# Attention and gated feed-forward on one core: values products in three bursts a pair, output copies a unit later, small writes and one multiplication moved on GpSimd

## Chip, cores and metric

One Trainium2 chip, one core of it. The metric is device time of one execution in microseconds (us), as the median of several runs; lower is better. TensorE is PE in the profile, VectorE DVE, ScalarE ACT, GpSimd POOL, and SyncE, which issues the DMAs, SP.

## What is computed

The reference, cut to what matters (4 batches, 8 heads, 576 positions, head size 64, all float32):

```python
scores = scale * q @ k.T + bias            # bias from a small network on relative positions
attn   = exp(scores - max); attn /= sum
x      = attn @ v                           # heads side by side: (4, 576, 512)
h      = relu(x @ w_in)
conv   = sum_k conv_w[k] * h shifted by k   # three taps along the sequence
out    = (h * sigmoid(conv)) @ w_out
```

## The kernel before, in words

Three stages follow each other: the bias network (until about 65 us), attention (65 to 297 us), and the feed-forward part. Nothing reorders the work: each engine runs its instructions in the order in which the Python code issues them, and waits on semaphores where data or a buffer is not ready.

Attention works on **pairs** n = 0 to 15: two heads of one batch. A pair has five **units**, 0 to 4, one for each tile of queries (`t`, in the loop also `ui`); unit 0 holds the first 64 queries of both heads, units 1 to 4 hold 128 queries of each head. The main loop counts all units as `u`. In one turn of it, the steps belong to three different units, so that each engine has work ahead:

- PE multiplies the scores of unit u + 2, one head after the other (`scores`, L349), into two PSUM buffers that take turns (`psS`). DVE adds the bias, takes the row minimum of the negated sum and writes it to SBUF (`reduce`, L360, with a small read of the accumulator, `nm`). A score buffer is free again when its reduction is done, and the second head's also serves, in units 1 to 4, for a few transposes (`side_transposes`, L408; L412 turns the row sums) that DVE copies out.
- ACT exponentiates unit u + 1 (`expo`, L374). After that `turned_sp` (L328) writes two columns of the same SBUF buffer under its second name `sr`, so that the next tenant of the buffer, three units on, has something to wait for.
- PE transposes unit u (`transposes`, L420), the two row halves of the tile into two of three PSUM buffers (`psT`). ACT copies one out, DVE the other (lines L88 and L91): into `ptx` for units 0 to 2 (X, 320 columns), into `pty` for units 3 and 4 (Y, 256 columns).
- PE multiplies the transposed tile with the values (`pv_parts`, L457). X and Y of a pair are five parts each, of two matmuls each, in one PSUM buffer (`psO`); the trace has two records for each matmul. The queue `fill` holds the parts, and `pv_share` says how many parts unit 0, 1, 2, 3 and 4 run after their transposes. Y of a pair is ready after its unit 4, so it is worked off in units 0 to 2 of the next pair; X in units 3 and 4. The last part of X or Y copies the output from PSUM to the tile `x` (ACT, L88).

Beside this, weights for the second part are narrowed: a raw tile is loaded, in odd `u` DVE shifts one word right (L97) and ACT scales the other (L99), in even `u` DVE joins them (L103) and POOL splits the result in two (L131, L132). Once a pair POOL multiplies the output of the pair before last by the inverse sums (`apply_norm`, L497), which come back from memory as the tile `rb`.

The lines that say how the parts are shared and what the last part does:

```python
pv_share = (2, 2, 1, 3, 2)
...
parts = len(fill) if u < 5 else pv_share[ui]
while fill and parts > 0:
    fill.popleft()()
    parts -= 1
...
if ui == 2 and n > 1:
    apply_norm(n - 2)
```

Of the kernel before, what the change touches and what calls it, by code (L numbers as in the profile page):

```python
# [9 lines left out]
F32 = mybir.dt.float32  # L10
F32R = mybir.dt.float32r
I32 = mybir.dt.int32
AF = mybir.ActivationFunctionType
# [6 lines left out]
def attention_ffn_kernel(  # L20
# [11 lines left out]
    nc = tc.nc  # L32
    B, S, DM = out.shape
    NP = qk.shape[1]
# [4 lines left out]
    P = 128  # L39
# [30 lines left out]
    x_p = pool(ctx, "x", B)  # L70
# [16 lines left out]
    def act(o, i):  # L87
        nc.scalar.activation(o, i, AF.Copy)  # L88
# [45 lines left out]
    with tc.manual_schedule():  # L134
# [134 lines left out]
        def bias_out(blk):  # L269
            nf, nr = reach(blk)  # L270
            n = max(nf, nr + 1)
            ps = bias_ps.pop(blk)
            st = sts[blk // 2 % 5].rearrange("p (b n) -> p b n", b=2)
            if n > 512:
                o, i = st[:, blk % 2:blk % 2 + 1], ps.rearrange("p (b a) x -> p b (a x)", b=1)
            else:
                o, i = st, ps
            fwd = nf > nr


            if n > 512 or blk % 2:
                k = relu_from(blk) - 3
                for oo, ii in (
                    (slice(nr, nr + nf), slice(0, nf)) if fwd else (slice(0, nr + 1), slice(nr, None, -1)),
                    (slice(0, nr), slice(nr, 0, -1)) if fwd else (slice(nr + 1, nr + nf), slice(1, nf)),
                ):
                    nc.scalar.activation(o[:, :, oo], i[:, :, ii], AF.Identity, bias=kv[:, k:k + 1], scale=inv_scale)  # L287
            if blk % 2 == 0:
                return
            at = 64 + (blk - 1) * P * BW - nr  # L290
            dst = bias_d[at:at + 2 * P * BW].rearrange("(b p c) -> p b c", b=2, c=BW)
            nc.sync.dma_start(dst[:, :, 0:nr + nf], st[:, :, 0:nr + nf])
# [14 lines left out]
        xb = {0: x0}  # L307
# [17 lines left out]

        def turned_sp(n, t):
            tile = sp_p.tile([P, 2 * S + 2], F32R, name="sr", tag=spt[n, t][1])
            nc.scalar.activation(tile[:, 2 * S:], pars[:, 0:2], AF.Copy)  # L328
            spt[n, t] = (tile, None)


# [105 lines left out]

        ops_t = {}
        waiting = {}

        def pv_parts(n, g):
            p, b = seq[n]

            waiting[n] = waiting.get(n, 0) + 1
            x0, width = (XW, YW) if g else (0, XW)

            def part(c):
                pt, vt = ptt[n, g], vts[n]
                if c == 0:
                    ops_t[n, g] = psO.tile([P, 512], F32, name="o")  # L450
                po = ops_t[n, g]
                for h in range(2):
                    if c == 4:
                        slot, blk = (9 if h else 4), 4
                    else:
                        slot = blk = 5 + c if h else c
                    nc.tensor.matmul(  # L457
                        po[D * h:D * h + D, 0:width], vt[:, slot, :], pt[:, blk, :],
                        start=(c == 0), stop=(c == 4),
                    )  # L460
                if c == 4:
                    del ptt[n, g]
                    waiting[n] -= 1
                    if b not in xb:
                        xb[b] = x_p.tile([P, NP, S], F32, name=f"x{b}", tag="x")
                    act(xb[b][:, p, x0:x0 + width], po[:, 0:width])

            return [lambda c=c: part(c) for c in range(5)]

        def invert(n):  # L470
            sm, r = sms.pop(n), rr_t[n % 2][:, 0:9]
            nc.vector.tensor_scalar(r, sm, 1e-9, None, op0=ALU.add)
            nc.vector.reciprocal(r, r)
# [120 lines left out]
        for i in range(NBLK):  # L594
            nxt = bias_hidden(i + 1) if i + 1 < NBLK else None
            bias_mm(i, hidden)
            if last:
                bias_out(*last)
            last = (i,)
            hidden = nxt  # L600
            if i % 8 == 6 % 8 and i >= 6:
                load_bias(0, (i - 6) // 8)
            if i == 1:
                load_v(0)
            if i == 16:
                load(1)
            if i == 20:
                load_v(1)
            if i % 8 == 13 % 8 and i >= 13:
                unit = unit_steps(*first[(i - 13) // 8])  # L610
            if unit:
                next(unit, None)
            if fill:
                fill.popleft()()
        bias_out(*last)
        load_bias(0, 4)
        while fill:
            fill.popleft()()
        for _ in unit:
            pass  # L620
        for u in range(2):
            for h in heads(flat[u][1]):
                reduce(scores(*flat[u], h), *flat[u], h)
            if u == 0:
                for h in heads(flat[0][1]):
                    expo(*flat[0], h)
                turned_sp(*flat[0])
        pv_share = (2, 2, 1, 3, 2)
        hs_ff = {}
        raw_w = {}  # L630
        job_steps = iter(())
# [3 lines left out]
        for u, (n, t) in enumerate(flat):  # L635
            p, b = seq[n]
            ui = units.index(t)
            sums = n - 1 if ui == 2 and n else None
            side = None
            if u + 2 < NU:  # L640
                for h in heads(flat[u + 2][1]):
                    if side is not None:
                        reduce(side, *flat[u + 2], 0)
                    side = scores(*flat[u + 2], h)
            if t:
                if side is None:
                    side = psS.tile([P, 2, 512], F32, name="s")
                side_transposes(side, n, t, sums)
            if u + 2 < NU:
                reduce(side, *flat[u + 2], h)  # L650
            if u + 1 < NU:
                for h in heads(flat[u + 1][1]):
                    expo(*flat[u + 1], h)
                turned_sp(*flat[u + 1])
            transposes(n, t, side, sums)
            next(job_steps, None)

# [4 lines that stand above are left out]
            next(job_steps, None)  # L662
            del spt[n, t]
            if u + 2 >= NU:
                f = u + 2 - NU
                hs_ff[0, f] = ffn_in(0, f)
            if u == 1 or n and ui == 2 and n + 2 < NSEQ:
                load(2 if u == 1 else n + 2)
            if u in conv_weights:
                conv_weights[u]()  # L670

            for at, do in ((u - 7, "load"), (u - 11, "split")):
                job = at // 2
                if at % 2 == 0 or not 0 <= job < 4 * KC + 2 * FE:
                    continue
                if job < 4 * KC:
                    src, dst = w_in[job // 4 * P:job // 4 * P + P], wi[job // 4]
                else:
                    src, dst = w_out[(job - 4 * KC) // 2 * P:(job - 4 * KC) // 2 * P + P], wo[(job - 4 * KC) // 2]
                cs = slice(job % 4 * 256, job % 4 * 256 + 256) if job < 4 * KC else slice(job % 2 * 256, job % 2 * 256 + 256)  # L680
                if do == "load":
                    raw_w[job] = (e_p if job % 3 else woe_p).tile([P, 256, 2], I32, name="raw_w", tag="h")
                    load_w(raw_w[job], src[:, cs])
                else:
                    job_steps = split_w_steps(e_p, dst[:, :, cs], raw_w.pop(job), ("cv", "cv"))
            if u + 2 < NU:
                n2, t2 = flat[u + 2]
                p2, b2 = seq[n2]
                if b2 == B - 1 and p2 + 1 < NP:
                    load_bias(p2 + 1, t2)  # L690
            if ui == (0 if n > 1 else 1) and n > 0:
                invert(n - 1)
            if ui == (2 if n > 1 else 3) and 1 <= n and n + 1 < NSEQ:
                load_v(n + 1)
            if ui == 3 and n > 0:
                store_sums(n - 1)
            if ui == 4 and n > 0:
                spread_sums(n - 1)
            if ends_group(n, t):
                fill.extend(pv_parts(n, t > 2))  # L700

            if ui == 2 and n > 1:
                apply_norm(n - 2)
            if n == NSEQ - 2 and ui > 1:
                x_parts(0, ui - 2)
            if n == NSEQ - 1 and ui == 0:
                x_parts(0, 3)
            if n == NSEQ - 1 and ui in (1, 2):
                load_wo(FE - 1 + ui)
        while fill:  # L710
            fill.popleft()()
        invert(NSEQ - 1)
        turn_sums(NSEQ - 1)
        apply_norm(NSEQ - 2)
# [200 lines left out]
```

## Time and profile before

| | |
|---|---|
| three runs | 502.59 us median, 502.55 to 504.32 |
| profiled execution, its own time | 501.91 us |
| its span, first to last instruction | 500.1 us |
| mean granted TensorE clock | 0.998 of full speed |
| PE, weight loads, DVE, ACT, POOL busy | 96%, 70%, 77%, 62%, 21% of the span |
| attention, 150 to 200 us: PE, DVE, ACT, POOL busy in 50 us | 49.57, 44.97, 42.44, 15.10 us |
| DMA engines' mean share in that stretch | 0.80 |
| chain that ended last | PE 87%, DVE 5%, ACT 5% |

The busy share of PE is no measure of how much of PE is used, since matmuls are pipelined and their ends are modelled. What can be read well is the start of each group: the time from one start to the next is what a group costs where PE doesn't wait. The sum of the profiled execution is made against its own 501.91 us, which lies 0.68 us under the median.

### The profile page before, as it was taken

To read this page: it belongs to the slowest core of one execution; us is meant where nothing else is said; L and a number is where in the kernel's file an instruction comes from. 1 tells how busy PE (TensorE), PEld (TensorE's weight loads), DVE (VectorE), ACT (ScalarE), POOL (GpSimd) and SP (SyncE) were. 2 spreads that over 40 slices of the span, in tenths; PEclk is the share of its full clock that TensorE was granted. 3 is DMA by queue.
4 is the path that set the end of the run, shared out by engine and by line. 5 is a ranking of instruction groups with operands and counts; after the bars stand their busy time and mean duration, and the time that the engine had idled before them with its cause. 6 is when DMAs were issued, how large, how long until landed. Compare 5 with 4: busy or idle time off the path is not lost.

```text
span 500.1 us, 11125 instructions
## 1 busy us (share of the span) xinstructions
PE 479.1 (96%) x4202; PEld 352.5 (70%) x4202; DVE 386.5 (77%) x875; ACT 311.1 (62%) x747; POOL 103.4 (21%) x121
## 2 busy tenths in 40 slices
PE   5988899999999999999999999899999999999994
PEld 3333256666666666666666689779988999899884
DVE  6999957888899988889898729974994299649900
ACT  5888877878888889888887736622632154126400
POOL 1000000103232313323336215620080005200000
PEclk9999999999999999999999999999999999999999
DMA  5779556488778977788751300002000200020011
GB/s 138 268 248 333 213 176 150 109 234 225 171 167 211 250 177 177 200 221 260 189 147 56 113 16 26 1 1 85 0 1 8 92 8 1 1 85 1 2 63 42
DMA packets 32703, 60.83 MB, mean 122 GB/s; under 512 B 5490, under 2 KB 12170, under 8 KB 32650
## 3 DMA queue, kind: packets, MB, share of 16 engines
q1 hardware_dynamic: 32506, 60.04, 42.2%
q8 instruction: 33, 0.54, 0.5%
q14 instruction: 20, 0.16, 0.1%
q10 hardware_dynamic: 144, 0.08, 0.1%
HBM read 44.12 MB, written 15.98 MB: 120 GB/s over the span
## 4 chain that ended last, share of the span: by engine, by line
PE 87%; DVE 5%; ACT 5%; issue 1%; DMA 1%; DVEq 0%; ACTq 0%
PE o L457 18%; PE s L518 17%; PE s L349 16%; PE tp L766 15%; PE tp L420 9%; PE s L261 6%; PE o L766 4%; ACT st L287 2%; DVE cv L741 2%; PE s L408 1%; DVE sp L360 1%; ACT y L240 1%; DMA pars<-in_par_dram 1%; ACT sp L374 1%; DVE cv L748 1%
## 5 line engine op out<-in xcount | busy, mean ns | idle before, releaser
L360 DVE CUSTOM_DVE_ANT_0 sp<-s,bt 128x576 f32<-128x576 f32 x144 | 104.2, 754 | 32.0 <-PE s L349 14.5
L374 ACT ACTIVATE sp<-sp,nm 128x576 f32<-128x576 f32 x144 | 109.9, 767 | 1.4 <-DVE nm L360 1.4
L518 PE MATMUL s<-xs,wi 128*128 128x288 f32 x768 | 103.8, 296 | 1.7 <-ACT h L530 1.7
L518 PEld LDWEIGHTS s<-xs,wi 128*128 128x128 f32 x768 | 102.8, 189 | 3.2 <-ACT h L530 2.0
L349 PE MATMUL s<-qk 64*128 64x288 f32 (+1 forms) x640 | 93.1, 431 | 1.8 <-DVE nm L360 1.1
L349 PEld LDWEIGHTS s<-qk 64*128 64x128 f32 (+1 forms) x640 | 46.8, 175 | 44.8 <-DVE nm L360 13.0
L766 PE MATMUL tp<-wo,g 128*128 128x512 f32 x288 | 70.5, 390 | 0.0
L420 PE MATMUL tp<-identr,sr 64*128 64x64 f32 x1184 | 64.3, 247 | 0.0
L741 DVE SCALAR_TENSOR_TENSOR cv<-h,cw,cv 128x575 f32<-128x575 f32 x64 | 60.6, 946 | 2.5 <-ACT cv L736 0.6
L766 PEld LDWEIGHTS tp<-wo,g 128*128 128x128 f32 x288 | 53.7, 188 | 11.6 <-DVE g L761 0.7
L420 PEld LDWEIGHTS tp<-identr,sr 64*128 64x128 f32 x1184 | 55.5, 136 | 5.7 <-issue 0.6
L457 PE MATMUL o<-ptx,vt 128*64 128x320 f32 x320 | 50.4, 443 | 1.3 <-ACT ptx L88 0.9
L261 PE MATMUL s<-y,pars 128*32 128x512 f32 (+8 forms) x352 | 46.5, 504 | 5.0 <-ACT st L287 2.2
L530 ACT ACTIVATE h<-s 128x576 f32<-128x576 f32 x32 | 20.8, 650 | 47.7 <-PE s L518 47.7
L497 POOL TENSOR_TENSOR x<-x,rb 128x576 f32<-128x576 f32 x16 | 23.6, 1473 | 128.6 <-ACT sp L374 94.2
L244 DVE TENSOR_SCALAR y<-tl,inv,nb 128x512 f32<-128x512 f32 (+8 forms) x116 | 49.9, 506 | 0.1
L457 PE MATMUL o<-pty,vt 128*64 128x256 f32 x320 | 44.2, 393 | 0.0
L261 PEld LDWEIGHTS s<-y,pars 128*32 128x32 f32 x352 | 16.4, 113 | 32.8 <-DVE y L244 17.4
L747 ACT ACTIVATE cv<-cv 128x576 f32<-128x576 f32 x32 | 21.8, 683 | 28.4 <-DVE cv L741 28.4
L91 DVE COPY ptx<-tp 128x256 f32<-128x256 f32 (+1 forms) x64 | 32.0, 500 | 1.4 <-PE tp L420 1.2
L131 POOL TENSOR_SCALAR xs<-x 128x576 fp32r<-128x576 f32 x16 | 14.8, 924 | 81.5 <-PE s L518 81.5
L88 ACT ACTIVATE ptx<-tp 128x256 f32<-128x256 f32 (+1 forms) x64 | 26.4, 438 | 7.9 <-PE tp L420 7.3
(75 smaller groups left out, 570.6 us busy)
## 6 DMA issues: line engine op xcount, KB each, us to landing
qk<-in_qk_dram SPq DMA_DIRECT2D x32, 320.0 KB
bt<-bias_d SPq DMA_DIRECT2D x32, 288.0 KB
bias_d<-st SPq DMA_DIRECT2D x14, 607.0 KB
qk<-in_qk_dram SPq DMA_DIRECT2D x32, 144.0 KB
rb<-r_d SPq DMA_DIRECT2D x32, 144.0 KB
out_dram<-o SPq DMA_DIRECT2D x17, 256.0 KB
raw_w<-in_moe_w_in_dram SPq DMA_DIRECT2D x16, 256.0 KB
raw_w<-in_moe_w_out_dram SPq DMA_DIRECT2D x12, 256.0 KB
```

The costliest lines, as they stand in the source:

```text
L88: nc.scalar.activation(o, i, AF.Copy)
L91: nc.vector.tensor_copy(o, i)
L244: nc.vector.tensor_scalar(y, dist[:, 0:n], inv[:, ig:ig + 1], nb1, op0=ALU.mult, op1=ALU.max)
L261: nc.tensor.matmul(ps[32 * j:32 * j + 32, a // 512 if n > 512 else blk % 2, 0:min(n - a, 512)], w2b, ys[j][:, a:min(n, a + 512)], start=Tr ...
L349: nc.tensor.matmul(ps[po, a, 0:HS], qt[rows, qo:qo + po.stop - po.start], qt[rows, KO + hh * HS:KO + hh * HS + HS], start=True, stop=True,)
L360: nc.vector.tensor_tensor_reduce(out=halves(spt[n, t][0][:, h]), in0=ps[:, :, 0:HS], in1=halves(bt[:, h]), op0=ALU.add, op1=ALU.min, scale ...
L374: exps[n, t, h] = nc.scalar.activation(sp[:, h], sp[:, h], AF.Exp, bias=nm[:, h:h + 1], scale=-1.0, accum_out=sms[n][:, col:col + 1],)
L420: tr = nc.tensor.transpose(ps[a][:, TL * s:TL * s + TL].bitcast(F32R), spf[ra, j:j + P], identr[ra, ra])
L457: nc.tensor.matmul(po[D * h:D * h + D, 0:width], vt[:, slot, :], pt[:, blk, :], start=(c == 0), stop=(c == 4),)
L518: nc.tensor.matmul(ps[:, a, 0:HS], wi[c][:, pw, cs], xss[b, c][:, px, a * HS:(a + 1) * HS], start=(i == 0), stop=(i == 3 * KC - 1),)
L741: nc.vector.scalar_tensor_tensor(out=cv[:, o:o + S - 1], in0=h[:, i:i + S - 1], scalar=cw[:, f, kk:kk + 1], in1=cv[:, o:o + S - 1], op0=AL ...
L766: nc.tensor.matmul(ps, lhs(f, gi), wo[f][:, wj, cs], start=(f == 0 and i == 0), stop=(f == FC - 1 and i == 2),)
```

## The change

Four edits. The output copy of X and Y is no longer issued by the last part, but put on a list that is worked off in the next unit, after ACT's exponentials and ahead of its copies of the transposes. The parts are shared as 0, 5, 0, 2, 3. The two columns of `sr` are written by POOL in place of ACT. POOL's multiplication is issued in an odd unit: in unit 2 for even pairs as before, in unit 3 for odd pairs.

```diff
         def turned_sp(n, t):
             tile = sp_p.tile([P, 2 * S + 2], F32R, name="sr", tag=spt[n, t][1])
-            nc.scalar.activation(tile[:, 2 * S:], pars[:, 0:2], AF.Copy)
+            nc.gpsimd.tensor_copy(tile[:, 2 * S:], pars[:, 0:2])
...
+        late = []
+        def outputs():
+            while late:
+                late.pop(0)()
...
                 if c == 4:
                     del ptt[n, g]
-                    waiting[n] -= 1
-                    if b not in xb:
-                        xb[b] = x_p.tile([P, NP, S], F32, name=f"x{b}", tag="x")
-                    act(xb[b][:, p, x0:x0 + width], po[:, 0:width])
+                    late.append(lambda: out_of_psum(po))
...
-        pv_share = (2, 2, 1, 3, 2)
+        pv_share = (0, 5, 0, 2, 3)
...
                     expo(*flat[u + 1], h)
                 turned_sp(*flat[u + 1])
+            outputs()
             transposes(n, t, side, sums)
...
-            if ui == 2 and n > 1:
+            if ui in (2, 3) and u % 2 and n > 1:
                 apply_norm(n - 2)
```

PE, units 0 to 2 of one pair, before (s is a score buffer, tp a buffer of transposes, o the output buffer; x4 counts matmuls):

```order
L349 MATMUL s<-qk 128x288 x4
L420 MATMUL tp<-identr,sr 128x64 x10
L457 MATMUL o<-pty,vt_107 64x256 x4
L349 MATMUL s<-qk 128x288 x4
L408 MATMUL s<-identr,sr 128x64 x2
L420 MATMUL tp<-identr,sr 128x64 x16
L457 MATMUL o<-pty,vt_107 64x256 x4
L349 MATMUL s<-qk 128x288 x4
L408 MATMUL s<-identr,sr 128x64 x2
L412 MATMUL s<-ident,rr_160 128x64 x2
L420 MATMUL tp<-identr,sr 128x64 x16
L457 MATMUL o<-pty,vt_107 64x256 x2
```

And the same units in the changed kernel:

```order
L349 MATMUL s<-qk 128x288 x4
L420 MATMUL tp<-identr,sr 128x64 x10
L349 MATMUL s<-qk 128x288 x4
L408 MATMUL s<-identr,sr 128x64 x2
L420 MATMUL tp<-identr,sr 128x64 x16
L462 MATMUL o<-pty,vt_107 64x256 x10
L349 MATMUL s<-qk 128x288 x4
L408 MATMUL s<-identr,sr 128x64 x2
L412 MATMUL s<-ident,rr_160 128x64 x2
L420 MATMUL tp<-identr,sr 128x64 x16
```

Units 0 and 2 go from their transposes straight to the next scores; the ten matmuls of Y stand together in unit 1.

POOL, from one multiplication of a pair to the next, before, with the semaphores that each waits for (DMAHW: a DMA):

```order
L497 TENSOR_TENSOR x_1532<-x_1532,rb 128x576 [waits DMAHW5_49,DMAHW3_49,DMAHW6_49,DMAHW2_49,Activation_49]
L131 TENSOR_SCALAR wi_743<-wu 128x256 [waits DVE_49]
L132 TENSOR_TENSOR wi_743<-wu,wi_743 128x256 [waits Pool_49]
L131 TENSOR_SCALAR wi_743<-wu 128x256 [waits DVE_49]
L132 TENSOR_TENSOR wi_743<-wu,wi_743 128x256 [waits Pool_49]
L497 TENSOR_TENSOR x_121<-x_121,rb 128x576 [waits DMAHW6_49,DMAHW5_49,Activation_49]
```

And in the changed kernel:

```order
L505 TENSOR_TENSOR x_1553<-x_1553,rb 128x576 [waits DMAHW5_49,DMAHW6_49,DMAHW3_49,DMAHW2_49]
L328 CAST sr<-pars 128x2 [waits Activation_49]
L131 TENSOR_SCALAR wi_743<-wu 128x256 [waits DVE_49]
L132 TENSOR_TENSOR wi_743<-wu,wi_743 128x256 [waits Pool_49]
L328 CAST sr<-pars 128x2 [waits PE_49,Activation_49]
L328 CAST sr<-pars 128x2 [waits Activation_49]
L131 TENSOR_SCALAR wi_743<-wu 128x256 [waits DVE_49]
L132 TENSOR_TENSOR wi_743<-wu,wi_743 128x256 [waits Pool_49]
L328 CAST sr<-pars 128x2 [waits PE_49,Activation_49]
L505 TENSOR_TENSOR x_121<-x_121,rb 128x576 [waits DMAHW6_49,DMAHW5_49]
```

The small writes stand between the multiplication and the splits, each behind ACT's exponentials of its unit; the multiplication stands behind a small write.

ACT, two units of one pair that hold the last part of Y, before:

```order
L374 ACTIVATE sp,sm<-sp,nm 128x576 x2
L328 ACTIVATE sr<-pars 128x2
L88 ACTIVATE ptx<-tp 128x8x64
L374 ACTIVATE sp,sm<-sp,nm 128x576 x2
L328 ACTIVATE sr<-pars 128x2
L88 ACTIVATE ptx<-tp 128x8x64
L88 ACTIVATE x_1532<-o 128x256
L99 ACTIVATE wu<-raw_w 128x256
```

And in the changed kernel:

```order
L374 ACTIVATE sp,sm<-sp,nm 128x576 x2
L88 ACTIVATE ptx<-tp 128x8x64
L374 ACTIVATE sp,sm<-sp,nm 128x576 x2
L88 ACTIVATE x_1553<-o 128x256
L88 ACTIVATE ptx<-tp 128x8x64
L99 ACTIVATE wu<-raw_w 128x256
```

The small writes are gone from ACT, and the output copy stands ahead of unit 2's copy of the transposes, where it stood behind it.

## Rows read from the trace of the kernel before

**Rows 1.** The page, busy time, share of the span and instructions

```profile
PE 479.1 (96%) x4202; PEld 352.5 (70%) x4202; DVE 386.5 (77%) x875; ACT 311.1 (62%) x747; POOL 103.4 (21%) x121
```

**Rows 2.** Timeline of PE, one pair: start, length, instruction, count of records

```profile
203.19 1.24 PE L349 MATMUL s<-qk 64*128 64x288 f32 x8
204.04 0.73 PE L420 MATMUL tp<-identr,sr 64*128 64x64 f32 x10
204.70 1.08 PE L457 MATMUL o<-pty,vt 128*64 128x256 f32 x8
205.72 1.24 PE L349 MATMUL s<-qk 64*128 64x288 f32 x8
...
207.56 1.08 PE L457 MATMUL o<-pty,vt 128*64 128x256 f32 x8
208.57 1.24 PE L349 MATMUL s<-qk 64*128 64x288 f32 x8
...
209.74 0.82 PE L420 MATMUL tp<-identr,sr 64*128 64x64 f32 x16
210.49 0.65 PE L457 MATMUL o<-pty,vt 128*64 128x256 f32 x4
211.07 0.72 PE L349 MATMUL s<-qk 64*64 64x288 f32 x8
...
211.80 0.83 PE L420 MATMUL tp<-identr,sr 64*128 64x64 f32 x16
212.56 1.83 PE L457 MATMUL o<-ptx,vt 128*64 128x320 f32 x12
...
217.40 1.24 PE L349 MATMUL s<-qk 64*128 64x288 f32 x8
```

**Rows 3.** Timeline of PE, first units of the loop, without values products until 80.19

```profile
70.23 0.81 PE L420 MATMUL tp<-identr,sr 64*128 64x64 f32 x16
...
70.87 1.40 PE L349 MATMUL s<-qk 64*128 64x288 f32 x7
...
73.98 0.76 PE L349 MATMUL s<-qk 64*128 64x288 f32 x4 [0.50 <-DVE nm L360]
...
74.60 0.82 PE L420 MATMUL tp<-identr,sr 64*128 64x64 f32 x16
...
80.19 2.38 PE L457 MATMUL o<-pty,vt 128*64 128x256 f32 x20
...
82.49 0.71 PE L349 MATMUL s<-qk 64*64 64x288 f32 x8
```

**Rows 4.** Timeline of DVE: end of a second head's reduction, and a copy of transposes

```profile
73.84 0.08 DVE L360 DVE_READ_ACCUMULATOR2_ANT nm<- 128x1 f32 x1
...
205.35 0.08 DVE L360 DVE_READ_ACCUMULATOR2_ANT nm<- 128x1 f32 x1
...
211.14 0.67 DVE L91 COPY ptx<-tp 128x512 f32<-128x512 f32 x1
...
219.68 0.08 DVE L360 DVE_READ_ACCUMULATOR2_ANT nm<- 128x1 f32 x1
```

**Rows 5.** Timeline of ACT, copies of transposes in unit 2 of two pairs

```profile
210.59 0.60 ACT L88 ACTIVATE ptx<-tp 128x512 f32<-128x512 f32 x1 [0.40 <-PE tp L420]
...
282.37 0.60 ACT L88 ACTIVATE ptx<-tp 128x512 f32<-128x512 f32 x1 [0.63 <-PE tp L420]
```

**Rows 6.** Timeline of PE, the last pair's unit 3

```profile
282.97 0.89 PE L420 MATMUL tp<-identr,sr 64*128 64x64 f32 x16
```

**Rows 7.** Instructions of one line: count, ns least/median/most, starts

```profile
L328 ACT ACTIVATE sr<-pars x80: 187/203/212, 28.4 to 284.9; 128x2 fp32r<-128x2 f32 x80
...
L97 DVE TENSOR_SCALAR wu<-raw_w x28: 271/286/1535, 108.7 to 262.9; 128x256 int32<-128x256 int32 x28
```

**Rows 8.** Timelines of PE and POOL, pair 8: unit 2's start, multiplication, split

```profile
179.61 1.24 PE L349 MATMUL s<-qk 64*128 64x288 f32 x8
...
187.03 1.41 POOL L497 TENSOR_TENSOR x<-x,rb 128x576 f32<-128x576 f32 x1 [5.43 <-DMA rb<-r_d]
188.41 0.41 POOL L131 TENSOR_SCALAR wi<-wu 128x256 fp32r<-128x256 f32 x1
```

More of the change, by code (lines that the diff above doesn't have):

```diff
@@ L462, in part, with out_of_psum @@
                     del ptt[n, g]
-                    waiting[n] -= 1
-                    if b not in xb:
-                        xb[b] = x_p.tile([P, NP, S], F32, name=f"x{b}", tag="x")
-                    act(xb[b][:, p, x0:x0 + width], po[:, 0:width])
+                    late.append(lambda: out_of_psum(po))
+            def out_of_psum(po):
+                waiting[n] -= 1
+                if b not in xb:
+                    xb[b] = x_p.tile([P, NP, S], F32, name=f"x{b}", tag="x")
+                act(xb[b][:, p, x0:x0 + width], po[:, 0:width])
             return [lambda c=c: part(c) for c in range(5)]
@@ L618, in attention_ffn_kernel @@
             fill.popleft()()
+        outputs()
         for _ in unit:
@@ L654, in attention_ffn_kernel @@
                 turned_sp(*flat[u + 1])
+            outputs()
             transposes(n, t, side, sums)
@@ L711, in attention_ffn_kernel @@
             fill.popleft()()
+        outputs()
         invert(NSEQ - 1)
```

## The prediction

> **What bounds the kernel now.** I read the page first: PE is busy for 96% of the span, no other engine for more than 77% [rows 1]. Busy time can hide waits, so I went on to PE's timeline in the middle of attention, and took the steps from one start to the next [rows 2]. The pair shown takes 217.40 - 203.19 = 14.21 us. In it every kind of group has a fixed step: the scores of two heads 0.85 to 0.87 us, sixteen transposes 0.75, ten 0.66, one part of Y 0.58 (211.07 - 210.49), two parts 1.02, three parts of X 1.77. No row of the pair carries a wait. So in attention a change pays only by what it takes from PE's own steps, and it loses whatever wait it brings in. The bias stage and the feed-forward part keep their orders.
>
> **What the bursts save.** Y stands in three bursts of 2, 2 and 1 parts: 1.02 + 1.01 + 0.58 = 2.61 us a pair. One burst of five parts is in the trace too, where the loop starts: 82.49 - 80.19 = 2.30 [rows 3]. One more part costs about 0.43, so each burst has about 0.15 of its own, and two bursts less save 0.31 us. X changes from 3 + 2 to 2 + 3 parts: nothing. A second saving lies in the units that lose their products: scores follow transposes after 0.64 (70.87 - 70.23) [rows 3], products after 0.75 [rows 2], so 0.11 in each of units 0 and 2, where PE may go on at once.
>
> **May it go on?** Units 0 and 1 first. A second head's scores need the buffer of the second head before, so they wait for its reduction. For the unit 0 at 203.19 this reduction's last read starts at 205.35, 2.16 us after the unit [rows 4]. The first units of the loop have no products either and show what follows: read at 73.84, scores at 73.98 with a wait on that very read [rows 3, 4], 0.14 later. DVE is idle ahead of unit 0's reductions and they can't start before their scores, so the read stays at 2.16. In the changed kernel the second head's scores of unit 1 would come at 0.85 + 0.66 + 0.43 (one head) = 1.94; they start at 2.16 + 0.14 = 2.30. From there 0.62 to the transposes (74.60 - 73.98), 0.75, and 2.30 for the five parts: unit 2 starts at 5.97 after unit 0, against 208.57 - 203.19 = 5.38 now. In every other pair the reduction is later: the unit at 217.40 has its read at 219.68, that is 2.28, and 6.09. Units 0 and 1 thus become longer by 0.59 or about 0.70.
>
> Units 2 to 4 now take 217.40 - 208.57 = 8.83. They lose one part with its burst (0.58) and 0.11. But unit 3's transposes need ACT's copy of unit 2's, which starts 0.85 after unit 2's transposes and takes 0.60 [rows 2, 5]: it ends 1.17 + 0.85 + 0.60 = 2.62 after unit 2's start, where PE would be at 1.17 + 0.64 + 0.73 = 2.54. The last pair has this today: its transposes at 282.97 start as the copy of 282.37 ends and last 0.89 instead of 0.83 [rows 5, 6]. I take 0.12 of wait. DVE's copy ends 2.57 + 0.67 = 3.24 after unit 2's start [rows 4] and is needed by X at about 3.4: free in one kind of pair, some 0.04 in the other. Units 2 to 4 become shorter by 0.57 or 0.53.
>
> The pair changes by +0.59 - 0.57 = **+0.02** or +0.70 - 0.53 = **+0.17** us. Seven pairs of the one kind and six of the other (2 to 14) give 7 x 0.02 + 6 x 0.17 = 1.2. In pair 15 unit 2's part of Y lies under that ACT copy already, so its loss saves nothing there, while units 0 and 1 grow as elsewhere: +0.6.
>
> **The other edits.** Output copies: ACT no longer waits for PE's last part ahead of its next exponentials. PE loses no wait by it, having none; Y's first part comes a whole unit after X's copy, X's first part one unit after Y's, so the one output buffer is free in time. 0. If ACT were late by more than half a us in unit 2, unit 3's transposes would show it next.
>
> Small writes: 80 of 0.203 us leave ACT [rows 7]; ACT isn't waited for but in the place just priced, and there its queue is empty. 0. POOL gets 80 writes, no such row being there: at least ACT's 0.20, at most the 0.41 of a split over 256 columns [rows 7, 8]; I take 0.20, since two columns are nearer to the first, so 16 us (at most 33) on an engine idle for 79% of the span. New is a wait: a unit's first reduction waits for the write that the buffer's last tenant got two units earlier. DVE has all of its reductions and copies behind that wait, and PE its scores.
>
> Multiplication: a shift (L97) has a median of 0.286 us and a most of 1.535 [rows 7]. The long ones stand beside a multiplication, so a meeting costs DVE up to 1.26 us. No wait of PE comes from it now, as DVE catches up in units that products lengthen. For odd pairs the multiplication now starts behind the small write of unit 3, for even pairs behind that of unit 2. I put 0 for odd pairs; even pairs are a rival. The DMAs keep their order, and SP's loads of values lose a wait for PE; 0, with at most 0.5 us to gain where a bias row came late.
>
> The Trainium skill (SBUF — State Buffer, Who interferes with whom) says that a VectorE instruction that uses both port pairs and a GpSimd one exclude each other, and that the second to issue waits for the whole of the first. The trace agrees, with the 1.535 above; by the rule alone, a move that follows no semaphore of DVE's clears nothing for certain, which is the third rival.
>
> Sum against the profiled execution: 501.91 + 1.2 + 0.6 = 503.7; the median of the runs lies 0.68 above that execution, so **504.4 us**, 0.4% above 502.59. Two runs can be told apart here from about 0.5%, 2.5 us. A reading of each step to 0.1 us, over 14 pairs, makes 502.0 to 506.5 the range of this case.
>
> **Rivals.**
> 1. The waits don't appear, because the reductions or the buffers are earlier than I read them. Then 14 pairs save 0.31, and 0.22 more if units 0 and 2 go on at once: 502.59 - 4.3 = 498.3, down to 495.2. For it: the savings themselves are rows. Against: the wait at 73.98 is exactly this one.
> 2. Slower: POOL's queue. The multiplication waits for the tile rb from memory, and the small writes now stand behind it. In pair 8 it started at 187.03, 7.42 us after unit 2's start, behind 5.43 of waiting for the DMA [rows 8]. It would end at 8.83 and the write of unit 3 at about 9.05 to 9.25; the next pair's first reduction wants it at 8.27 + 0.80 = 9.07. So it decides as soon as rb comes a few tenths later than now. Pairs 4 and 12 follow the same bias loads. With rb 2 us later all three hold DVE for 2 us: 504.4 + 6 = 510.4, with 1 us 507.4. The Trainium skill (TensorE: Matmul & The Clock Gate, Part 1, Architectural detail) states that GpSimd takes its instructions strictly in order; no run here shows yet what that does to small writes. Against: today's lateness just fits.
> 3. Even pairs' multiplication meets the shift in unit 2, which is now 0.7 us shorter. DVE is then 1.26 late, the next reduction, its side copy and unit 4's second scores with it; about half reaches PE, an estimate: 7 x 0.6 = 4.2, so 508.6, or 506 if three of them meet. For it: 1.535. Against: the meeting hangs on a few tenths of us.
>
> **How the numbers follow.** Forecast 0.50, of which a third lies above 505.1 (0.5%) and the rest within; rival 1 0.25, all of it faster; rival 2 0.10, all slower; rival 3 0.15, half of it slower. That makes faster 0.25, same 0.50 x 2/3 + 0.07 = 0.40, slower 0.17 + 0.10 + 0.08 = 0.35. The range 497.5 to 508.0 takes in the forecast's own, the nearer half of rival 1, and the nearer prices of rivals 2 and 3; it leaves out two savings together and a POOL queue that is held for long.
>
> **What would show it.** Right: PE's burst of x20 in unit 1 with a step of 2.30; in unit 1 scores of x4 apart from the first x4, with a wait on DVE nm of 0.3 to 0.5 us; transposes of unit 3 lengthened by about 0.1; pairs of 14.2 to 14.4 us; no small write on ACT. Wrong: pairs of 13.7 to 13.9 (rival 1); a reduction waiting for POOL (rival 2); shifts of 1.5 us in even pairs and a wait of unit 4's scores (rival 3).

## The result and the profile after

The changed kernel takes 506.48 us in the median (505.49 to 510.19), the kernel before beside it 502.57 (501.15 to 507.47): a ratio of 1.0075, interval 1.0055 to 1.0095. Slower by 0.75%, inside the range given, and on the side with a chance of 0.35, not the likeliest of the three; the forecast's own part of it, 502.0 to 506.5, holds it by 0.02. The profiled execution took 505.81 with a span of 504.0, 3.9 more than before. Cut at starts that both traces have, these 3.9 us lie here:

| stretch | before | after | difference |
|---|---|---|---|
| start to the first values burst after the bias stage | 60.94 | 61.17 | +0.23 |
| from there to the second unit 3 (82.49, 82.96) | 21.55 | 21.79 | +0.24 |
| 13 pairs, unit 3 to unit 3 | 185.50 | 186.78 | +1.28 |
| from the last of these to the last pair's first X burst | 15.86 | 16.47 | +0.61 |
| from there to the last burst of Y | 10.61 | 11.74 | +1.13 |
| from there to the end | 205.64 | 206.05 | +0.41 |

The 13 pairs hold one thing that is no part of the change: in either trace a row of the bias comes late once, and DVE waits for it.

```profile
180.84 0.76 DVE L360 CUSTOM_DVE_ANT_0 sp<-s,bt 128x576 f32<-128x576 f32 x1 [0.54 <-DMA bt<-bias_d]
```

```profile
240.04 0.76 DVE L360 CUSTOM_DVE_ANT_0 sp<-s,bt 128x576 f32<-128x576 f32 x1 [0.95 <-DMA bt<-bias_d]
```

Before, its pair took 14.75 in place of 14.23; after, 14.48 in place of 14.36. Without these 0.52 and 0.12 the 13 pairs cost 1.28 + 0.52 - 0.12 = 1.68, or 0.13 each. All of them now take 14.35 to 14.48.

First PE's timeline in the pair that answers to [rows 2] (columns as there):

```profile
204.17 1.24 PE L349 MATMUL s<-qk 64*128 64x288 f32 x8
205.03 0.72 PE L420 MATMUL tp<-identr,sr 64*128 64x64 f32 x10
205.91 1.44 PE L349 MATMUL s<-qk 64*128 64x288 f32 x8 [0.15 <-DVE nm L360]
206.96 0.41 PE L408 MATMUL s<-identr,sr 64*128 64x64 f32 x2
...
207.95 2.38 PE L462 MATMUL o<-pty,vt 128*64 128x256 f32 x20
210.26 1.24 PE L349 MATMUL s<-qk 64*128 64x288 f32 x8
...
211.43 0.81 PE L420 MATMUL tp<-identr,sr 64*128 64x64 f32 x16
212.17 0.72 PE L349 MATMUL s<-qk 64*64 64x288 f32 x8
...
218.54 1.24 PE L349 MATMUL s<-qk 64*128 64x288 f32 x8
```

The burst of five stands in unit 1 with the step forecast, 210.26 - 207.95 = 2.31. Ahead of it the scores wait for `nm`. The forecast had one wait, of 0.36, ahead of the second head; the trace has two smaller ones. The first head starts at 205.91, 0.14 after the first read of `nm` below, and the two heads then take 206.96 - 205.91 = 1.05, where the prediction has 0.85 to 0.87. The second read ends the longer path, as forecast. Units 0 and 1 take 6.09 (5.38 before), units 2 to 4 8.28 (8.83 before). The saving of 0.11 behind unit 2's transposes did not come: 212.17 - 211.43 is 0.74.

DVE in the same unit 0 answers to [rows 4]:

```profile
205.08 0.76 DVE L360 CUSTOM_DVE_ANT_0 sp<-s,bt 128x576 f32<-128x576 f32 x1 [1.04 <-PE s L349]
205.77 0.08 DVE L360 DVE_READ_ACCUMULATOR2_ANT nm<- 128x1 f32 x1
...
206.44 0.08 DVE L360 DVE_READ_ACCUMULATOR2_ANT nm<- 128x1 f32 x1
```

The second read starts 206.44 - 204.17 = 2.27 after the unit. Before, every other pair had 2.16; now the 13 pairs have 2.26 to 2.28. In pair 15 it comes 2.72 after the unit (2.98 before), since DVE stands in a long instruction there, beside one of GpSimd; DVE, GpSimd and PE:

```profile
276.07 1.47 DVE L103 SCALAR_TENSOR_TENSOR w<-u,w 24x128 int32<-24x128 int32 x1
```

```profile
275.98 1.41 POOL L132 TENSOR_TENSOR xs<-x,xs 128x576 fp32r<-128x576 f32 x1
```

```profile
278.27 1.43 PE L349 MATMUL s<-qk 64*128 64x288 f32 x8 [0.59 <-DVE nm L360]
```

At the end of attention, PE's last burst of Y, and ACT ahead of it, first before and then after:

```profile
294.46 2.38 PE L457 MATMUL o<-pty,vt 128*64 128x256 f32 x20
```

```profile
291.22 0.44 ACT L88 ACTIVATE x<-o 128x320 f32<-128x320 f32 x1 [0.67 <-PE o L457]
```

```profile
297.95 2.38 PE L462 MATMUL o<-pty,vt 128*64 128x256 f32 x20 [1.07 <-ACT x L88]
```

```profile
296.92 0.65 ACT L538 ACTIVATE h<-s 128x576 f32<-128x576 f32 x1 [4.54 <-PE s L526]
297.47 0.43 ACT L88 ACTIVATE x<-o 128x320 f32<-128x320 f32 x1
```

X's copy is issued behind the feed-forward part's first relu copies (L538), which wait for 24 matmuls. Y needs the output buffer and waits 1.07. Before, the copy stood ahead of the relu copies and Y waited for nothing; the prediction had no such wait.

Last, the lines that answer to [rows 7]:

```profile
L97 DVE TENSOR_SCALAR wu<-raw_w x28: 271/284/745, 109.2 to 264.7; 128x256 int32<-128x256 int32 x28
...
L328 POOL CAST sr<-pars x80: 178/186/418, 28.2 to 287.0; 128x2 fp32r<-128x2 f32 x80
```

The long shifts are gone in this trace (at most 0.745, 1.535 before), and a small write takes GpSimd 0.19.

### The profile page after: what moved, and what is told of

It is laid out like the page before. It is cut to its first block, busy times and chain, and to the rows that moved or that the text cites. A ratio compares the mean times of both kernels' runs of the same rounds, so it can differ in the third digit from the quotient of the medians.

```text
span 504.0 us, 11129 instructions
## 1 busy us (share of the span) xinstructions
PE 478.6 (95%) x4202; PEld 354.2 (70%) x4202; DVE 381.3 (76%) x875; ACT 295.7 (59%) x667; POOL 117.2 (23%) x201
## 4 chain that ended last, share of the span: by engine, by line
PE 82%; DVE 8%; ACT 4%; issue 2%; DMA 2%; POOL 0%; SPq 0%; DVEq 0%
PE s L526 17%; PE o L462 15%; PE tp L778 15%; PE s L349 14%; PE tp L420 8%; PE s L261 6%; PE o L778 4%; DVE sp L360 3%; ACT st L287 2%; DVE cv L753 1%; DVE cv L760 1%; PE s L408 1%; DMA bt<-bias_d 1%; DMA pars<-in_par_dram 1%; ACT y L240 1%
## 5 line engine op out<-in xcount | busy, mean ns | idle before, releaser
L360 DVE CUSTOM_DVE_ANT_0 sp<-s,bt 128x576 f32<-128x576 f32 x144 | 104.0, 754 | 39.6 <-PE s L349 26.0
L349 PE MATMUL s<-qk 64*128 64x288 f32 (+1 forms) x640 | 95.5, 435 | 4.5 <-DVE nm L360 3.2
L753 DVE SCALAR_TENSOR_TENSOR cv<-h,cw,cv 128x575 f32<-128x575 f32 x64 | 59.4, 928 | 2.5 <-ACT cv L748 0.6
L538 ACT ACTIVATE h<-s 128x576 f32<-128x576 f32 x32 | 20.8, 650 | 49.4 <-PE s L526 49.4
L328 POOL CAST sr<-pars 128x2 fp32r<-128x2 f32 x80 | 16.1, 202 | 142.7 <-ACT sp L374 142.7
L462 PE MATMUL o<-pty,vt 128*64 128x256 f32 x320 | 38.1, 384 | 1.1 <-ACT x L88 1.1
```

Of the source, the lines that this page charges most:

```text
L349: nc.tensor.matmul(ps[po, a, 0:HS], qt[rows, qo:qo + po.stop - po.start], qt[rows, KO + hh * HS:KO + hh * HS + HS], start=True, stop=True,)
L360: nc.vector.tensor_tensor_reduce(out=halves(spt[n, t][0][:, h]), in0=ps[:, :, 0:HS], in1=halves(bt[:, h]), op0=ALU.add, op1=ALU.min, scale ...
L462: nc.tensor.matmul(po[D * h:D * h + D, 0:width], vt[:, slot, :], pt[:, blk, :], start=(c == 0), stop=(c == 4),)
L753: nc.vector.scalar_tensor_tensor(out=cv[:, o:o + S - 1], in0=h[:, i:i + S - 1], scalar=cw[:, f, kk:kk + 1], in1=cv[:, o:o + S - 1], op0=AL ...
```

## The experiments

Theory: the longer pair is PE's wait in unit 1, the end is the late copy, the rest is free. Rivals: the small writes, the late copies or the multiplication lengthen the pair.

| run | median, us | ratio to before (interval) | pairs, us |
|---|---|---|---|
| e1_share | 508.03 | 1.0107 (1.0072 to 1.0142) | 14.55 and 14.70 in turn from the third on |
| e2_late | 519.2 | 1.0318 (1.0283 to 1.0352) | 15.01 and 15.67 in turn from the third on |
| e5_tail | 504.99 | 1.0045 (1.0029 to 1.0061) | 14.34 to 14.39, two 15.43, 14.51 |
| e6_cover | 503.97 | 1.0034 (1.0010 to 1.0058) | 14.08 to 14.12, two 15.45, 15.85 |
| e3_actw | 504.67 | 1.0049 (1.0028 to 1.0069) | 14.25 and 14.36 in turn from the third on |
| e11_early | 504.64 | 1.0047 (1.0033 to 1.0062) | 14.23 to 14.26, one 14.71 |
| e4_mult | 502.99 | 1.0000 (0.9980 to 1.0020) | 14.22 to 14.24, two 14.45, 14.58 |
| e8_norm0 | 524.57, one run | | 14.34 to 14.38, four 16.18 to 22.45 |
| e7_best | 502.73 | 1.0029 (0.9998 to 1.0060) | 14.09 to 14.11, three 14.44 to 14.60 |
| e9_bias | 501.04 | 0.9953 (0.9923 to 0.9983) | 14.09 to 14.11 |
| e10_bias | 501.86 | 0.9984 (0.9965 to 1.0004) | 14.22 to 14.25 |
| e12_lean | 501.12 | 0.9960 (0.9941 to 0.9978) | 14.09 to 14.11 |

Pairs are the 13 steps from unit 3 to unit 3 of the profiled execution, as in the table above. The runs stand below in the order of the argument.

### One part alone: shares, late copies

```diff
-        pv_share = (2, 2, 1, 3, 2)
+        pv_share = (0, 5, 0, 2, 3)
```

> The kernel before with the shares 0, 5, 0, 2, 3 alone. Theory (PE waits in unit 1 for the second reduction of unit 0, and that wait belongs to the shares): pairs of 14.36 us as in the changed kernel, up to 14.5 if the output copy, still issued at once, holds ACT ahead of unit 3's transposes; no long wait at the end of attention; 505.0, at most 506.9. Rival (the small writes on GpSimd or the late copies bring the longer pair, the shares by themselves only save bursts): pairs of 13.9, about 499.

The rival falls: the shares alone lengthen the pair, and by more than with the other edits. The theory was too low as well. PE and then ACT in unit 3:

```profile
199.73 0.72 PE L349 MATMUL s<-qk 64*64 64x288 f32 x8
...
200.92 0.83 PE L420 MATMUL tp<-identr,sr 64*128 64x64 f32 x15 [0.22 <-ACT ptx L88]
...
202.91 1.24 PE L349 MATMUL s<-qk 64*128 64x288 f32 x8
```

```profile
197.93 0.38 ACT L88 ACTIVATE x<-o 128x256 f32<-128x256 f32 x1 [1.01 <-PE o L457]
...
200.29 0.58 ACT L88 ACTIVATE ptx<-tp 128x512 f32<-128x512 f32 x1
```

ACT's output copy, issued at once, waits 1.01 us for the five-part burst, and the exponentials behind it come late as well. So ACT's copy of unit 2's transposes starts 2.48 after that unit, where the changed kernel has 2.02, and unit 3 takes 3.18 in place of 2.75.

The late copies alone are the change without its other three edits.

> The kernel before with the late output copies alone. Theory: pairs stay at 14.23; only the last output copy of X comes late, behind the first copy of the feed-forward part on ACT, and the last burst of Y waits for it by 1.07 us as in the changed kernel; 503.6. Rival (late copies lengthen the pair): pairs of 14.36, 505.3. Third case: no wait at the end either, 502.6.

All three cases fell. With the old shares each group's first part stands one unit behind the other group's last part, in the same output buffer, and PE waits twice a pair:

```profile
197.31 0.87 PE L462 MATMUL o<-pty,vt 128*64 128x256 f32 x6 [0.34 <-ACT x L88]
...
205.89 1.83 PE L462 MATMUL o<-ptx,vt 128*64 128x320 f32 x12 [0.63 <-ACT x L88]
```

So these two edits only go together: each alone costs more than both (e3_actw has both: 14.25 and 14.36). A unit without products between Y's last part and X's first makes the room for a copy that comes a unit later. Unit 0 needs none: in e12_lean at the end, X's last part still stands in unit 4 and Y's first in unit 0, and no burst of the pair shown waits.

### The end, and the wait in unit 1

```diff
             if u + 2 >= NU:
+                outputs()
                 f = u + 2 - NU
```

> The changed kernel with the late copies worked off ahead of the feed-forward step in the last two units. Theory: the wait of 1.07 us ahead of the last burst of Y goes and the rest stays; 505.4. Rival (the wait is hidden by the relu copies that follow and comes back ahead of the next feed-forward group): 506.5.

The wait is gone: X's copy starts at 294.25, behind its own burst, and Y's burst waits for nothing. From the last pair's first X burst (286.87) to the last burst of Y (297.48) it is 10.61 again. The median is 1.5 lower, though this trace has a pair of 15.43 with a late reduction in it.

```diff
-        pv_share = (0, 5, 0, 2, 3)
+        pv_share = (1, 4, 0, 2, 3)
```

> The changed kernel with the shares 1, 4, 0, 2, 3: one burst more for each pair, which by itself costs PE 0.15 us. Theory: one part in unit 0 puts the second scores of unit 1 at 2.5 us after unit 0, past the 2.4 at which the buffer comes free; the wait goes, unit 0 and 1 take 5.82 in place of 6.09, and the pair 14.10: 506.5 - 14 x 0.26 = 502.8. Rival (the longer pair has nothing to do with that wait): pairs of 14.36 + 0.15 = 14.5, 508.6.

The pairs are 14.10: a burst more, and 0.26 less, so the wait in unit 1 was the price. Two pairs stand out by 3.1 us together; the last section comes to them.

### A tenth of a microsecond in a reduction

The small writes back on ACT, all else as in the changed kernel:

> The changed kernel with the small writes back on ACT. Theory (ACT has room ahead of every copy that PE waits for once the output copies are late): pairs of 14.36, 506.5. Rival (the room on ACT is what the small writes gave): unit 3's transposes wait 0.1 to 0.2 us longer for ACT's copy of unit 2, pairs of 14.5, 508.5. Third case (the small writes on GpSimd held DVE's reductions): pairs of 14.23, 504.6.

None of the three cases: the pairs take 14.25 and 14.36 in turn. In the shorter ones unit 0's first reduction starts 0.80 after its scores, in the longer 0.91, and so it was in the kernel before. The instruction lists show what goes with it. Unit 0's first reduction on DVE, with the semaphores it waits for, and its start after the scores in the trace:

```
before, behind L103         [waits PE_49]                 0.80
before, pairs 4, 8, 12      [waits DMAHW3_49,PE_49]       0.80 or 0.81
before, behind L97          [waits PE_49,Activation_49]   0.91
changed, all but these      [waits PE_49,Pool_49]         0.91
```

A second semaphore listed behind PE's, though long given, goes with a start 0.11 later. The changed kernel's view of L360, cut to 204.5 to 205.5 us, shows what stands between:

```profile
L360 DVEq EVENT_SEMAPHORE  x1: 21/21/21, 205.0 to 205.0; - x1
L360 DVE CUSTOM_DVE_ANT_0 sp<-s,bt x1: 758/758/758, 205.1 to 205.1; 128x576 f32<-128x576 f32 x1
```

With two semaphores DVE runs an instruction more. It stands at 205.0, 0.8 after the scores at 204.17, where a reduction that waits for PE alone starts; the reduction itself follows at 205.08. Where L103 has waited for ACT already the reduction need not, which is why it alternates before. The next run moves GpSimd's semaphore to an instruction of its own:

```diff
             tile = sp_p.tile([P, 2 * S + 2], F32, name="sp", tag=tag)
+            nc.vector.memset(tile[:, 2 * S:], 0.0)
```

> The changed kernel with one write of two columns on DVE ahead of each unit's first reduction; it takes the wait for GpSimd, so that the reduction waits for PE alone. Theory (a reduction that waits for PE and then for a second engine starts 0.11 us later, 0.91 in place of 0.80 after the scores, and the wait of PE in unit 1 grows by that): all reductions of unit 0 at 0.80, all pairs 14.25; 506.5 - 13 x 0.11 = 505.0. Rival (the small writes cost by GpSimd's traffic, or the first reduction is late for another reason): 0.91 and 14.36 stay, 506.5; or the write itself lengthens DVE's chain in the units where DVE is not idle, 507.

```profile
203.42 0.06 DVE L318 MEMSET sp<- 128x2 f32 x1
204.52 0.76 DVE L361 CUSTOM_DVE_ANT_0 sp<-s,bt 128x576 f32<-128x576 f32 x1 [1.04 <-PE s L350]
```

That unit's scores start at 203.71, so the reduction comes at 0.81. All pairs are 14.23 to 14.26 but one with a late bias row, with GpSimd's writes still in place. The small writes thus cost by the semaphore that the reduction waits for, not by GpSimd's work.

### GpSimd: the multiplication

The multiplication's edit alone, in the kernel before:

> The kernel before with GpSimd's multiplication in the odd unit alone. Theory: shifts of 1.3 to 1.5 us are gone or rarer, pairs stay at 14.23 since PE never waited for them; 502.5. Rival (the meetings cost PE something that the trace does not name): 501.

```profile
L97 DVE TENSOR_SCALAR wu<-raw_w x28: 271/284/1536, 109.4 to 263.3; 128x256 int32<-128x256 int32 x28
```

No difference in time. Nor are the long shifts gone: four of 1.16 to 1.54 are left. By itself the edit does not place the multiplication clear of them. In the changed kernel the small writes stand ahead of it too, and even there nothing holds it clear: e11_early has a shift of 1.325. The start follows no semaphore of DVE's, as the third rival said. The price that rival put on a meeting with a shift does not show here: pairs with a long shift take no more.

```diff
-            if ui in (2, 3) and u % 2 and n > 1:
+            if ui == 0 and n > 1:
```

> The changed kernel with the multiplication issued in unit 0. Theory (GpSimd works strictly in its order, so the small writes of units 1 and 2 stand behind a multiplication that waits for rb, and DVE's reductions two units later behind them): in pairs 4, 8 and 12, where rb comes 11 to 13 us after unit 0, DVE and then PE are held for some 4 to 6 us; 506.5 + about 14 = 520. Rival (GpSimd or DVE get by without the write): 506.5.

The pair of 16.18 is another matter, a bias row for which DVE waited 2.82 us (126.52); the other three are held by the multiplication. GpSimd, DVE and PE in the first of these:

```profile
132.97 1.40 POOL L505 TENSOR_TENSOR x<-x,rb 128x576 f32<-128x576 f32 x1 [14.06 <-DMA rb<-r_d]
134.31 0.18 POOL L328 CAST sr<-pars 128x2 fp32r<-128x2 f32 x1
```

```profile
134.53 0.76 DVE L360 CUSTOM_DVE_ANT_0 sp<-s,bt 128x576 f32<-128x576 f32 x1 [5.38 <-POOL sr L328]
```

```profile
135.65 1.33 PE L349 MATMUL s<-qk 64*128 64x288 f32 x4 [3.19 <-DVE pty L91]
```

The Trainium skill (TensorE: Matmul & The Clock Gate, Part 1, Architectural detail) says that GpSimd takes its instructions strictly in order; this trace agrees, with DVE's 5.38 us behind the multiplication's 14.06. This is the second rival, seen: a multiplication that waits for memory holds the small write, that the reduction, that the scores. Not all of the 8.1 us that this pair is longer is the wait itself: behind it, from 136 to 142 us, the granted clock was 0.50. In the changed kernel the longest such wait was 5.12 (245.66), and no reduction waited behind it: this rival's margin was there, and it held.

### A version that beats both

e7_best has two parts in unit 0 and the mended end:

> The changed kernel with the shares 2, 3, 0, 2, 3 and the late copies ahead of the feed-forward step in the last two units. Theory: two parts in unit 0 cover the wait as one did in e6_cover, pairs of 14.10; the wait at the end (1.07) is gone; where the last bias row of a group of pairs comes late it costs what it did in e6_cover. 504.0 - 1.1 = 502.9, the kernel before within 0.3%. Rival (the parts ahead of unit 1 push DVE's copies and bring another wait): pairs of 14.2 or more, 504.

As expected, and the bias row of pair 8 is late again. In the code the last bias row of a pair's loads stands on SP behind the loads of queries and keys of the same unit. e9_bias issues it ahead of them:

```diff
+            if u + 2 < NU:
+                n2, t2 = flat[u + 2]
+                p2, b2 = seq[n2]
+                if b2 == B - 1 and p2 + 1 < NP:
+                    load_bias(p2 + 1, t2)
             if u == 1 or n and ui == 2 and n + 2 < NSEQ:
                 load(2 if u == 1 else n + 2)
```

> e7_best with the bias rows issued on SP ahead of the 928 KB of queries and keys and of the raw weights of the same unit. Theory (the row that comes late in pair 8 is late because it stands behind these loads): DVE's wait for the bias row in pair 8 goes, with it PE's wait behind it and the stretch of half clock that followed it in e6_cover; about 501.3. Rival (the row is late because its buffer comes free late, or the memory is busy whatever the order): as e7_best, 502.9.

> The kernel before with that order of the bias rows alone. Theory: the wait of 0.54 us of DVE in pair 8 and PE's longer pair there (14.75 in place of 14.23) go, and the slower ones of its runs come nearer to its fastest; 501.6. Rival: no change, 502.2.

In the traces both hold: neither has a late bias row past 75 us, all pairs are even, no run of either is above 503.25 (the kernel before beside them has 508.49), and e9_bias is faster than the kernel before, 0.9953 (0.9923 to 0.9983). In the kernel before the order alone is worth at most 0.35%, and its interval takes in no change.

> e9_bias with the small writes and the multiplication as in the kernel before, so only the shares 2, 3, 0, 2, 3, the late copies and the order of the bias rows. Theory: where PE does not wait in unit 1, neither edit on GpSimd bears on it: pairs of 14.10, 501.0 as e9_bias. Rival (ACT needs the room, or the meetings of multiplication and shift tell in the shorter pair): pairs of 14.2 or more, 502.5.

```profile
201.87 1.24 PE L349 MATMUL s<-qk 64*128 64x288 f32 x8
...
203.38 1.08 PE L462 MATMUL o<-pty,vt 128*64 128x256 f32 x8
204.40 1.24 PE L349 MATMUL s<-qk 64*128 64x288 f32 x8
...
206.25 1.52 PE L462 MATMUL o<-pty,vt 128*64 128x256 f32 x12
207.70 1.24 PE L349 MATMUL s<-qk 64*128 64x288 f32 x8
...
215.98 1.24 PE L349 MATMUL s<-qk 64*128 64x288 f32 x8
```

The second scores, 0.86 after 204.40, wait for nothing; units 0 and 1 take 5.83. The same time as e9_bias, with shifts of up to 1.53 us in it: neither edit on GpSimd earns anything here.

## Why the prediction was right, and where it was not

- **The wait in unit 1** was forecast at its place and size: 0.59 or 0.70 for units 0 and 1, measured 0.71 in the pair shown. Shown by e6_cover, which takes it away by filling unit 0.
- **Two kinds of pair.** The term of +0.02 was mis-sized. It kept the read of every other pair at 2.16, saying that it can't move; the small write's semaphore moved it to 2.27. Those seven pairs cost as much as the others, and the 13 cost 1.68 in place of 1.2. The term "small writes: 0" was wrong by that, shown by e11_early: with the semaphore off the reduction the pairs take 14.25, which is the +0.02 of the sum.
- **Units 2 to 4** came out at -0.55 in the pair shown and -0.57 in the one ahead of it (8.27 in place of 8.84), forecast -0.57 and -0.53. That is luck: two terms cancelled. The 0.11 saved behind unit 2's transposes was 0.01 at most, and the 0.12 of wait for ACT's copy was 0.04 in the pair shown and 0 in the other (unit 3's step from transposes to products, 0.80 or 0.76).
- **Pair 15:** forecast 0.6, measured 0.61, and this is luck too. By PE's timeline units 0 and 1 grew by 1.03 there (6.52 in place of 5.49), not by 0.6, since the second read came at 2.72. Before, it came at 2.98, behind products that covered it; the forecast took the pair as one like the others. And the rest up to X's burst, which the forecast left as it was, became shorter by 0.44 (3.59 in place of 4.03).
- **Output copies: 0** failed at the end of attention, where 1.1 us were missed. The argument followed the output buffer through the loop and not through the last two units, where ACT's queue holds feed-forward work. In the loop it holds, but through the shares alone (e2_late).
- **Multiplication: 0** held, e4_mult.
- **Rival 1** (bursts without waits) did not come in the changed kernel; with the wait covered, one burst less saves 0.13 a pair (e12_lean). **Rival 2** is real and had its margin, e8_norm0. **Rival 3** did not come in the 13 pairs; the meeting in pair 15 is one of its kind, of other instructions than it named.

The forecast of 504.4 was low by 2.1 us. By the table of stretches, 1.13 of it is the wait at the end, and 0.88 stands in three stretches where the sum had nothing: 0.23, 0.24 and 0.41. The 13 pairs add only 0.08, because the late bias rows hid 0.40 of what they missed, which is luck again. Of the 0.24, some 0.2 is the same semaphore: the first two waits for `nm` in that stretch are 0.48 and 0.29 where they were 0.38 and 0.18, and e3_actw and e11_early have 0.38 or 0.39 and 0.18 again. What the 0.41 us behind the last burst of Y and the 0.23 at the start are, was not tried.

## What to carry to other kernels

Where an engine runs without waits, a burst that is saved must be paid for by cover somewhere: put beside each group of work that goes how soon the next one needs another engine's answer, and leave just so much there. When copies or releases are made later, follow their queue to the last turn of the loop too, where something else stands in it. And a semaphore added to an instruction on the critical chain can have a price even when it was given long ago, here 0.11 us; an earlier instruction of the same engine, one with time, can take it.

## What was not expected of the hardware

A second semaphore behind the late one costs a reduction 0.11 us (0.91 against 0.80); one for a DMA, listed ahead of PE's, costs none (0.81). If the instruction that DVE runs ahead of the reduction takes the semaphore listed first, it holds PE's late one in the first case and the DMA's early one in the second, which fits both. Whether the place in the list or the engine decides was not tried apart.

A short idle of PE can cost more than itself. In e6_cover a bias row was 2.09 us late, and PE then idle for 1.29; DVE and PE:

```profile
182.11 0.76 DVE L360 CUSTOM_DVE_ANT_0 sp<-s,bt 128x576 f32<-128x576 f32 x1 [2.09 <-DMA bt<-bias_d]
```

```profile
182.93 0.81 PE L349 MATMUL s<-qk 64*64 64x288 f32 x8 [1.29 <-DMA r_d<-rt]
```

And the stretches behind it (length, busy time of PE, PEld, DVE, ACT and POOL with instructions, the granted clock of PE, DMA share, GB/s):

```profile
182.90:184.00 1.10, 1.07 (x16) 0.63 (x16) 1.10 (x5) 1.09 (x3) 0.00 (x0) 1.00 0.14 47
184.00:185.00 1.00, 1.00 (x18) 0.79 (x16) 1.00 (x3) 0.90 (x3) 0.00 (x0) 0.77 0.70 174
185.00:186.00 1.00, 1.00 (x6) 0.47 (x4) 1.00 (x4) 0.79 (x2) 0.00 (x0) 0.50 0.63 233
...
187.00:188.00 1.00, 1.00 (x4) 0.77 (x6) 0.00 (x0) 0.00 (x0) 0.32 (x1) 0.52 0.79 128
188.00:189.00 1.00, 1.00 (x20) 0.84 (x16) 0.67 (x1) 0.00 (x0) 1.00 (x1) 1.00 0.90 243
```

The clock fell from 2.4 to 1.2 GHz more than a microsecond after PE had gone back to work, for some 3.5 us, and the next pair took 15.85 in place of 14.10. In e5_tail, after an idle of 1.00 us, it stayed at 1.00. The late row of 2.09 cost 1.35 + 1.75 = 3.1 us in all. So the same order of loads cost half a microsecond in the profiled execution of the kernel before, 1.2 in e7_best's (a wait of 1.24, three pairs longer by 0.34 to 0.50) and 3.1 in this one. Why the row is later in one execution than in another stays open.
